# Attention from the fifth tile on: high and low halves of a head in one product, quadrants added at eviction

## The chip, the cores and the metric

The kernel runs on one core of one Trainium2 chip. The metric is the device time of one execution in microseconds. A core has a matrix engine (TensorE, in the rows PE, with PEld for its weight loads), a vector engine (VectorE, DVE), a scalar engine (ScalarE, ACT), GpSimd (POOL) and a sync engine that issues transfers (SyncE, SP). They run their own instruction streams and wait for one another through semaphores. Matrix products land in PSUM, which has eight banks of 2 KB per partition.

## What is computed

Three layers over 2304 tokens (4 sequences of 576) with 512 channels. The inputs of the dense layer come in 64-bit words. Cut to what matters here:

```python
scores = (q @ k.T) / 8            # 8 heads of 64 channels, causal window of 128 tokens
scores = where(mask, scores + bias, -1e9)
attn = exp(scores - scores.max(-1))
attn = attn / (attn.sum(-1) + 1e-9)
x = heads_to_channels(attn @ v)   # 2304 x 512
r = maximum(x @ w_in, 0)          # dense layer, 2048 hidden columns
x = (s * r * r + b) @ w_out
# then 8 experts of 1024 columns, the best two of each token, weighted and summed
```

The change concerns `attn @ v`.

## The kernel before

Attention works in 18 tiles of 128 tokens. A tile has four units, one for each pair of heads. A unit's tokens look at their own block of 128 keys and, if the sequence has one, the block ahead of it, so that most units have two key blocks and the first of a sequence has one (`blocks`). For each unit `qk` computes scores and probabilities, `ptr` transposes the probabilities into the PSUM tile `tp` and copies them to SBUF, and `av` multiplies them by V. `evac` copies the product, which has channels on the partitions, into `xh` and `xl`, from which the dense layer reads.

Operands that need precision are kept as a high part `h` and a low part `l` in a reduced 32-bit type, and a product is made of three: high by high, high by low, low by high. From tile 4 on (`FX`) attention does so for V: `split_v` makes the high part of V on ScalarE (L309) and the low part on GpSimd, into blocks `vb`; `ptr` makes the high probabilities `pth` on ScalarE (L366) and the low ones `ptl` on VectorE (L368). In `av` the stationary operand is a pair of heads, 128 channels of V, and the moving operand is the 256 probabilities of both heads of one block. Half of the result is of no use: the channels of head 0 under the probabilities of head 1 and the reverse.

```python
mm += [(so, h, th)] if ti < FX else [(so, h, th), (so, h, tl), (so, l, th)]
```

So one unit takes six matmuls of 128x256 (L382), three where it has one block. One PSUM bank `av` holds two units; there is one such bank. After the second unit `evac` takes the two useful quadrants: two copies on ScalarE (L391, 64x256) give `xh`, and two subtractions on VectorE (`low`, L118) give `xl`.

The dense layer works in nine chunks of 256 tokens, each in pairs of 256 hidden columns: `l1` (L457) reads `xh` and `xl` and makes `hp`, VectorE and ScalarE turn it into `gh` and `gl` (L465, L469), `l2` (L500) sums into the PSUM tiles `o`. Attention is woven between these matmuls. `marks` sets the pace: tiles 0 and 1 stand ahead of the first chunk, tiles 2 and 3 ahead of the second, and each chunk that follows must find its two tiles done. The first two chunks run in halves, and tiles 4 and 5 have four pairs of hidden columns to run in; later ones have a whole chunk. Two names of the router also stand in the orders below: `lp` (L532, gate) and `r_u`, `r_e` (its softmax).

Instructions are written in this program order. A scheduler in the framework sorts them for each engine when the program is built, by priority, estimated durations and free buffers; on the chip each engine runs its row in that order. The buffers that matter: PSUM has one bank for `tp`, one for `av`, two for scores `sp`, two for `hp`, two for `o`. In SBUF `pth` has one buffer, `ptl` two, which the weight conversion's `z` (L125) shares, `vb` has four, and the pool `u2k` has two for `g` of the dense layer and, in the first chunk, for the residual tiles `x` (L510) and `xt`.

The conversion of the dense layer's weights from 64-bit words (`conv1` to `conv3`, tiles `w`, `z`, `wih`, `wil`, `woh`, `wol`) runs on ScalarE and VectorE in the first 138 us.

## Time and profile before

| what | us |
|---|---|
| median of three runs | 1101.35 |
| lowest and highest | 1100.8, 1103.46 |
| the profiled execution | 1102.03 |
| its span (first to last instruction) | 1100.3 |
| TensorE busy in the span | 1063.5 |
| VectorE busy | 587.6 |
| ScalarE busy | 538.0 |
| GpSimd busy | 283.7 |

The profile is of one execution. Its time is 1.7 us more than its span. Busy time is the sum of instructions in work; TensorE's matmuls overlap, so what a matmul takes from the span is the distance from its start to the next start, not its length in the row. A line such as L382 is that of the kernel above.

### The profile page before, as it was taken

What the parts mean: (1) busy time and instruction counts of PE and PEld (TensorE: products, weight loads), DVE (VectorE), ACT (ScalarE), POOL (GpSimd) and SP (SyncE); (2) the same over time, 40 slices, a digit from 0 to 9 for tenths busy, and PEclk for the clock granted to TensorE, in tenths of its full rate; (3) what the DMA queues carried; (4) which work ended last, traced back from release to release, by engine and by line L of the source; (5) the groups of instructions that cost most, each with busy time, mean ns of one, the idle gap of its engine ahead of it and who ended that gap; (6) DMA issues with size and microseconds to landing.
All of it is one profiled execution on the core that took longest, in us unless ns stands there. A gap on an engine that the chain in (4) does not pass through costs nothing. (4 is left out here: it accounts for less than half of the span.)

```text
span 1100.3 us, 16721 instructions
## 1 busy us (share of the span) xinstructions
PE 1063.5 (97%) x6219; PEld 914.9 (83%) x6219; DVE 587.6 (53%) x1531; ACT 538.0 (49%) x1080; POOL 283.7 (26%) x265
## 2 busy tenths in 40 slices
PE   6899989999999999999999899999999999999997
PEld 3678878998999999999998787878888888887875
DVE  5999968767566676757455345242241421515140
ACT  4897667566566666555452145252342422424241
POOL 2000225324214242323001523323213032140223
PEclk9999999999999999999999999999999999999999
DMA  8965421011001111010233436455344343444212
GB/s 236 276 186 177 142 88 55 30 30 54 25 29 30 49 31 49 21 49 2 90 122 96 87 92 183 113 139 110 86 126 84 115 113 70 127 93 136 48 14 38
DMA packets 53779, 100.16 MB, mean 91 GB/s; under 512 B 12340, under 2 KB 23736, under 8 KB 53688
## 3 DMA queue, kind: packets, MB, share of 16 engines
q1 hardware_dynamic: 41784, 76.87, 22.8%
q0 software_dynamic: 11904, 22.08, 10.8%
q8 instruction: 57, 0.93, 0.4%
q14 instruction: 34, 0.28, 0.1%
HBM read 78.28 MB, written 23.78 MB: 93 GB/s over the span
## 5 line engine op out<-in xcount | busy, mean ns | idle before, releaser
L457 PE MATMUL hp<-xh,wih 128*128 128x256 f32 x576 | 168.0, 292 | 0.7 <-ACT wih L139 0.7
L457 PE MATMUL hp<-xl,wih 128*128 128x256 f32 x576 | 164.4, 285 | 0.4 <-DVE xl L118 0.4
L457 PE MATMUL hp<-xh,wil 128*128 128x256 f32 x576 | 164.2, 285 | 0.4 <-DVE wil L118 0.4
L785 PE MATMUL ys<-woh,wih 128*128 128x512 f32 x512 | 160.1, 393 | 0.2 <-ACT wih L732 0.2
L717 POOL DMA_INDIRECT xg<-x2d,ix x48 | 47.7, 993 | 316.8 <-PE xp L57 277.5
L804 ACT ACTIVATE yo<-ys,ls 128x512 f32<-128x512 f32 x46 | 31.2, 689 | 178.2 <-issue 147.2
L500 PE MATMUL o<-woh,gh 128*128 128x512 f32 x288 | 116.6, 406 | 0.0
L500 PE MATMUL o<-woh,gl 128*128 128x512 f32 x288 | 113.7, 395 | 0.2 <-DVE gl L469 0.2
L457 PEld LDWEIGHTS hp<-xh,wih 128*128 128x128 f32 x576 | 110.2, 191 | 3.8 <-ACT wih L139 1.1
L457 PEld LDWEIGHTS hp<-xl,wih 128*128 128x128 f32 x576 | 110.4, 192 | 3.2 <-DVE xl L118 1.9
L500 PE MATMUL o<-wol,gh 128*128 128x512 f32 x288 | 112.8, 392 | 0.0
L457 PEld LDWEIGHTS hp<-xh,wil 128*128 128x128 f32 x576 | 110.4, 192 | 1.0 <-DVE wil L118 0.6
L785 PEld LDWEIGHTS ys<-woh,wih 128*128 128x128 f32 x512 | 95.1, 188 | 19.2 <-ACT wih L732 0.5
L740 PE MATMUL hp<-xh,wih 128*128 128x512 f32 (+1 forms) x288 | 107.9, 375 | 3.2 <-DVE wil L733 1.3
L740 PE MATMUL hp<-xl,wih 128*128 128x512 f32 (+1 forms) x288 | 107.5, 373 | 2.1 <-PEq L766 0.9
L740 PE MATMUL hp<-xh,wil 128*128 128x512 f32 (+1 forms) x288 | 106.7, 370 | 1.2 <-PEq L766 0.6
L785 PE MATMUL ys<-woh,wil 128*128 128x512 f32 x256 | 100.0, 391 | 0.1
L805 POOL DMA_INDIRECT out_dram<-yo,ix x48 | 79.9, 1665 | 67.5 <-ACT yo L804 53.7
L118 POOL TENSOR_TENSOR ql<-rows,qd 64x256 fp32r<-64x256 f32 x52 | 39.5, 760 | 199.8 <-PE sp L325 138.9
L732 ACT ACTIVATE wih<-hp 128x512 fp32r<-128x512 f32 x64 | 37.9, 593 | 104.4 <-PE hp L740 104.2
L337 ACT ACTIVATE pr<-pr,st 128x256 f32<-128x256 f32 (+1 forms) x144 | 70.3, 489 | 29.6 <-DVE st L335 27.5
L733 DVE SCALAR_TENSOR_TENSOR wil<-hp,wih 128x512 fp32r<-128x512 f32 x64 | 44.1, 689 | 74.1 <-ACT wih L732 74.0
(181 smaller groups left out, 2269.6 us busy)
## 6 DMA issues: line engine op xcount, KB each, us to landing
raw<-in_moe_w_dram SPq DMA_DIRECT2D x64, 512.0 KB, 4.1
w<-in_moe_w_in_dram SPq DMA_DIRECT2D x16, 512.0 KB, 4.5
w<-in_moe_w_out_dram SPq DMA_DIRECT2D x16, 512.0 KB, 4.3
x2d<-x SPq DMA_DIRECT2D x22, 256.0 KB, 2.0
rows<-in_q_dram SPq DMA_DIRECT2D x18, 256.0 KB, 2.7
out_dram<-zero SPq DMA_DIRECT2D x18, 256.0 KB, 4.6
rows<-in_k_dram SPq DMA_DIRECT2D x16, 256.0 KB, 2.6
rows<-in_v_dram SPq DMA_DIRECT2D x14, 256.0 KB, 2.6
```

The costliest lines, as they stand in the source:

```text
L118: eng.tensor_tensor(out=dl, in0=x, in1=dh.bitcast(F32), op=OP.subtract)
L337: x_ = nc.scalar.activation(t[:, c], t[:, c], AF.Exp, bias=st[:, 0, e:e + 1], scale=-1.0, accum_out=st[:, 1, e:e + 1])
L457: nc.tensor.matmul(h[:, fi, :], a[:, kk, fs], bb[:, kk, cs], start=m == 0, stop=m == 3 * KD - 1)
L500: nc.tensor.matmul(o, a[:, ts], bb[:, f, :], start=i == i0 and m == 0, stop=i == i1 and m == 5)
L717: nc.gpsimd.indirect_dma_start(out=x, out_offset=None, in_=x2d, in_offset=bass.IndirectOffsetOnAxis(ap=LS[e, j][1], axis=0))
L732: nc.scalar.activation(dh, p, AF.Relu)
L733: nc.vector.scalar_tensor_tensor(out=dl, in0=p, scalar=0.0, in1=dh.bitcast(F32), op0=OP.max, op1=OP.subtract)
L740: nc.tensor.matmul(o, a[:, kk, fs], xt(z, c0, c1)[:, kk, :], start=m == 0, stop=m == 3 * KD - 1)
L785: nc.tensor.matmul(o, ht(z, j * 128, j * 128 + 128)[:, f // 2, f % 2], b[:, f, :], start=m == 0, stop=m == 3 * KF - 1)
L804: nc.scalar.activation(yo, y, AF.Copy, scale=wt)
L805: st = nc.gpsimd.indirect_dma_start(out=out, out_offset=bass.IndirectOffsetOnAxis(ap=ix, axis=0), in_=yo, in_offset=None, bounds_check=NT ...
```

## The change

From tile 4 on the operands are laid out by head. A block `vb` holds for each head its 64 high and 64 low columns next to one another, and a block `ptz` holds for each head the 128 high and 128 low probabilities next to one another. One matmul of a head and a key block then has 128 stationary columns (high and low V) and 256 moving ones (high and low probabilities). Its result has four quadrants: high by high, high by low, low by high, and low by low. A unit has two heads, so it takes four such matmuls with two blocks and two with one. It fills a PSUM bank by itself.

The eviction adds the quadrants. ScalarE copies two of them (L401, L402) into a scratch tile `ev`, VectorE adds high by high to the first (L403), then adds the sums into the first columns of the same PSUM bank, one head to each half of the partitions (L405, two instructions), ScalarE copies the result to `xh` (L406), and VectorE makes `xl` (L118). This runs for each unit. Low by low is among the quadrants that are added; before it was left out.

`ev` comes out of the pool `u2k`. `ptz`, the early tiles' `pth` and the conversion's `z` share three buffers. V's blocks are two of 4 KB in place of four of 2 KB, and the early tiles load their V in pairs into one such block.

```diff
-        z = x["z"] = ap.tile([128, 512], F32, name="z", tag="ptl", bufs=2).rearrange("p (k c) -> p k c", k=lo.shape[1])
+        z = x["z"] = ap.tile([128, 512], F32, name="z", tag="pz", bufs=3).rearrange("p (k c) -> p k c", k=lo.shape[1])
...
-            t = vblock(F32).rearrange("p (h d) -> p h d", d=D)
+            if ti % 2 == 0:
+                V["raw"] = vblock(F32).rearrange("p h z d -> p (h z d)").rearrange("p (a h d) -> p a h d", a=2, d=D)
+            t = V["raw"][:, ti % 2]
...
-        return ap.tile([128, DM], dt, name="vb", tag="vb", bufs=4)
+        return ap.tile([128, H, 2, D], dt, name="vb", tag="vb", bufs=2)
 
     def halve_v(ti, r):
-        V[ti] = (vblock(F32R), vblock(F32R))
-        nc.scalar.activation(V[ti][0], r, AF.Copy)
-        low(nc.gpsimd, V[ti][1], r, V[ti][0])
+        V[ti] = vblock(F32R)
+        nc.scalar.activation(V[ti][:, :, 0, :], r, AF.Copy)
+        low(nc.gpsimd, V[ti][:, :, 1, :], r, V[ti][:, :, 0, :])
...
-        th = ap.tile([128, 2, 2, 128], F32 if ti < FX else F32R, name="pth", tag="pth")
-        tl = ap.tile([128, 2, 2, 128], F32R, name="ptl", tag="ptl", bufs=2) if ti >= FX else None
         pt = P.pop(u)
         bl = blocks(ti)
         for so in bl:
             for e in range(2):
                 turn(tp[:, so, e, :], pt[e][:, so * 128:so * 128 + 128])
-        s = slice(0, 2) if len(bl) == 2 else slice(bl[0], bl[0] + 1)
-        nc.scalar.activation(th[:, s], tp[:, s], AF.Copy)
-        if tl is not None:
-            nc.vector.tensor_tensor(out=tl[:, s], in0=tp[:, s], in1=th[:, s].bitcast(F32), op=OP.subtract)
-        PT[u] = (th, tl)
+        if ti < FX:
+            th = ap.tile([128, 2, 2, 128], F32, name="pth", tag="pz", bufs=3)
+            s = slice(0, 2) if len(bl) == 2 else slice(bl[0], bl[0] + 1)
+            nc.scalar.activation(th[:, s], tp[:, s], AF.Copy)
+            PT[u] = th
+            return
+        PT[u] = {}
+        for so in bl:
+            x = PT[u][so] = ap.tile([128, 2, 2, 128], F32R, name="ptz", tag="pz", bufs=3)
+            nc.scalar.activation(x[:, :, 0], tp[:, so], AF.Copy)
+            nc.vector.tensor_tensor(out=x[:, :, 1], in0=tp[:, so], in1=x[:, :, 0].bitcast(F32), op=OP.subtract)
...
     def av(u):
         ti, p = divmod(u, NP)
-        th, tl = PT.pop(u)
-        if p % 2 == 0:
-            AV[ti, p // 2] = pp.tile([128, 2, 2, 128], F32, name="av", tag="av")
-        o = AV[ti, p // 2]
-        mm = []
-        for so in blocks(ti):
-            h, l = V[ti if so == tiles[ti].so else ti - 1]
-            mm += [(so, h, th)] if ti < FX else [(so, h, th), (so, h, tl), (so, l, th)]
-        for i, (so, a, bb) in enumerate(mm):
-            nc.tensor.matmul(o[:, p % 2], a[:, p * 128:(p + 1) * 128], bb[:, so], start=i == 0,
-                             stop=i == len(mm) - 1)
+        t = PT.pop(u)
+        if ti >= FX or p % 2 == 0:
+            AV[ti, p if ti >= FX else p // 2] = pp.tile([128, 2, 2, 128], F32, name="av", tag="av")
+        o = AV[ti, p if ti >= FX else p // 2]
+        bl = blocks(ti)
+        vs = [V[ti if so == tiles[ti].so else ti - 1] for so in bl]
+        n = len(bl) - 1
+        if ti < FX:
+            for i, so in enumerate(bl):
+                nc.tensor.matmul(o[:, p % 2], vs[i].rearrange("p h d -> p (h d)")[:, p * 128:(p + 1) * 128], t[:, so],
+                                 start=i == 0, stop=i == n)
+            return
+        for e in range(2):
+            for i, so in enumerate(bl):
+                nc.tensor.matmul(o[:, e], vs[i][:, 2 * p + e], t[so][:, e], start=i == 0, stop=i == n)
 
     def evac(ti, ph):
         o = AV.pop((ti, ph))
+        d = (ti * 128 + CH) % RING
+        if ti >= FX:
+            ev = u2k("ev").rearrange("p (z e q) -> p z e q", z=2, e=2)[0:64]
+            nc.scalar.activation(ev[:, 0], o[0:64, :, 1, :], AF.Copy)
+            nc.scalar.activation(ev[:, 1], o[64:128, :, 0, :], AF.Copy)
+            nc.vector.tensor_tensor(out=ev[:, 0], in0=o[0:64, :, 0, :], in1=ev[:, 0], op=OP.add)
+            for e in range(2):
+                nc.vector.tensor_tensor(out=o[64 * e:64 * e + 64, 0, 0, :], in0=ev[:, 0, e], in1=ev[:, 1, e], op=OP.add)
+            nc.scalar.activation(xh[:, ph, d:d + 128], o[:, 0, 0, :], AF.Copy)
+            low(nc.vector, xl[:, ph, d:d + 128], o[:, 0, 0, :], xh[:, ph, d:d + 128])
+            return
         ps = slice(2 * ph, 2 * ph + 2)
...
-            if p2 % 2:
-                add(lambda t2=t2, ph=p2 // 2: evac(t2, ph), need=(t2 * 128) // CH - 2,
+            if p2 % 2 or t2 >= FX:
+                add(lambda t2=t2, ph=p2 if t2 >= FX else p2 // 2: evac(t2, ph), need=(t2 * 128) // CH - 2,
```

On TensorE, where tile 4 ends and tile 5 begins (`o` is the dense layer's sum, `hp` its hidden values and `gh`, `gl` the same later, `sp` scores, `tp` transposes, `lp` the gate), before:

```order
L57 MATMUL tp<-ident,pr 128x128 x4
L457 MATMUL hp<-xh,wil 128x256
L457 MATMUL hp<-xh,wih 128x256
L457 MATMUL hp<-xl,wih 128x256
L457 MATMUL hp<-xh,wil 128x256
L500 MATMUL o<-woh,gh 128x512
L500 MATMUL o<-wol,gh 128x512
L500 MATMUL o<-woh,gl 128x512
L500 MATMUL o<-woh,gh 128x512
L500 MATMUL o<-wol,gh 128x512
L500 MATMUL o<-woh,gl 128x512
L382 MATMUL av<-pth,vb 128x256
```

and after:

```order
L394 MATMUL av<-ptz,vb 128x256 x4
L553 MATMUL lp<-wg,xt 128x16 x4
L57 MATMUL tp<-ident,pr 128x128 x4
L394 MATMUL av<-ptz,vb 128x256 x4
L325 MATMUL sp_119<-k_1518,qd 128x256
L327 MATMUL sp_119<-k_1518,ql 128x256
L521 MATMUL o<-woh,gh 128x512
```

Before, these rows stand between the last matmul of tile 4's last product and the first one of tile 5's first, which is the last row here: four transposes, four first-layer and six second-layer matmuls. After, the first row is tile 4's last product and the fourth tile 5's first: four gate matmuls and four transposes part them.

On VectorE, the second unit of tile 10 in the steady stretch (`xl` is the low part for the dense layer, `g` and `gl` are its hidden values), before:

```order
L469 SCALAR_TENSOR_TENSOR gl<-g,sb_c,gh 128x512
L535 COPY lg<-lp 128x16
L118 TENSOR_TENSOR xl<-av,xh 64x2x128 x2
L535 COPY lg<-lp 128x16
L465 SCALAR_TENSOR_TENSOR g<-hp,g 128x512
L547 TENSOR_SCALAR r_u<-r_e 128x16
L549 SCALAR_TENSOR_TENSOR r_e<-r_u,r_e 128x16
L368 TENSOR_TENSOR ptl<-tp,pth 128x512
```

and after:

```order
L556 COPY lg<-lp 128x16
L403 TENSOR_TENSOR ev<-av,ev 64x256
L405 TENSOR_TENSOR av<-ev 64x128 x2
L118 TENSOR_TENSOR xl<-av,xh 128x128
L556 COPY lg<-lp 128x16
L486 SCALAR_TENSOR_TENSOR g<-hp,g 128x512
L568 TENSOR_SCALAR r_u<-r_e 128x16
L570 SCALAR_TENSOR_TENSOR r_e<-r_u,r_e 128x16
L375 TENSOR_TENSOR ptz<-tp,ptz 128x2x128
```

Two subtractions have become three additions and one subtraction in a row of the engine, and the low probabilities `ptl` of both blocks have become two instructions `ptz`.

## Rows read from the trace of the kernel before

**Rows 1.** The page's busy times: busy us (share) x instructions of each engine
```profile
PE 1063.5 (97%) x6219; PEld 914.9 (83%) x6219; DVE 587.6 (53%) x1531; ACT 538.0 (49%) x1080; POOL 283.7 (26%) x265
```

**Rows 2.** Stretches: length, busy us (count) per engine PE PEld DVE ACT POOL, clock, DMA, GB/s
```profile
0.00:140.00 140.00, 124.55 (x651) 96.41 (x652) 121.73 (x315) 103.42 (x234) 19.91 (x32) 0.98 0.68 201
140.00:196.00 56.00, 52.10 (x359) 46.09 (x360) 41.46 (x143) 37.82 (x89) 22.20 (x22) 1.00 0.23 73
196.00:504.00 308.00, 306.58 (x2148) 283.04 (x2147) 203.90 (x667) 184.76 (x417) 99.14 (x100) 1.00 0.12 34
```

**Rows 3.** Timeline, TensorE: start, length us, engine, line, operation, tiles, elements
```profile
264.02 0.39 PE L500 MATMUL o<-woh,gl 128*128 128x512 f32 x1
264.25 0.28 PE L382 MATMUL av<-pth,vb 128*128 128x256 f32 x1
...
264.85 0.28 PE L382 MATMUL av<-pth,vb 128*128 128x256 f32 x1
264.97 0.28 PE L457 MATMUL hp<-xh,wih 128*128 128x256 f32 x1
```

**Rows 4.** Groups by line and shape: xcount | busy us, mean ns | idle before, releaser
```profile
L368 DVE TENSOR_TENSOR ptl<-tp,pth 128x512 fp32r<-128x512 f32 x52 | 35.8, 689 | 32.3 <-ACT pth L366 31.4
L366 ACT ACTIVATE pth<-tp 128x512 fp32r<-128x512 f32 x52 | 31.0, 596 | 53.0 <-PE tp L57 52.9
L118 DVE TENSOR_TENSOR xl<-av,xh 64x256 fp32r<-64x256 f32 x72 | 30.2, 420 | 13.0 <-ACT xh L391 12.2
L391 ACT ACTIVATE xh<-av 64x256 fp32r<-64x256 f32 x72 | 26.9, 374 | 5.0 <-PE av L382 4.1
L125 ACT ACTIVATE z<-w 128x512 f32<-128x512 f32 x32 | 21.5, 671 | 10.0 <-DMA w<-in_moe_w_in_dram 5.3 <-DVE w L133 3.6 <-DMA w<-in_moe_w_out_dram 1.1
L368 DVE TENSOR_TENSOR ptl<-tp,pth 128x256 fp32r<-128x256 f32 x4 | 1.7, 420 | 1.3 <-ACT pth L366 1.3
L366 ACT ACTIVATE pth<-tp 128x256 fp32r<-128x256 f32 x4 | 1.5, 382 | 4.8 <-PE tp L57 4.8
```

**Rows 5.** Timeline, evacuations of the steady stretch; [idle before <-releaser] in us
```profile
256.69 0.28 PE L382 MATMUL av<-pth,vb 128*128 128x256 f32 x1
...
258.62 0.77 ACT L391 ACTIVATE xh<-av 64x256 fp32r<-64x256 f32 x2
...
259.41 0.86 DVE L118 TENSOR_TENSOR xl<-av,xh 64x256 fp32r<-64x256 f32 x2 [2.18 <-ACT xh L391]
...
378.41 0.28 PE L382 MATMUL av<-pth,vb 128*128 128x256 f32 x1
...
439.64 0.28 PE L382 MATMUL av<-pth,vb 128*128 128x256 f32 x1
...
439.96 0.77 ACT L391 ACTIVATE xh<-av 64x256 fp32r<-64x256 f32 x2
...
440.76 0.86 DVE L118 TENSOR_TENSOR xl<-av,xh 64x256 fp32r<-64x256 f32 x2 [0.57 <-ACT xh L391]
```

**Rows 6.** Stretches in the place where tiles 4 and 5 run
```profile
148.00:160.00 12.00, 11.81 (x87) 10.75 (x85) 8.32 (x21) 5.35 (x14) 2.51 (x3) 1.00 0.14 45
160.00:172.00 12.00, 12.00 (x88) 10.97 (x89) 8.56 (x33) 10.20 (x25) 5.67 (x5) 1.00 0.13 45
172.00:184.00 12.00, 11.60 (x82) 10.03 (x82) 11.67 (x57) 7.53 (x21) 4.55 (x5) 1.00 0.09 24
```

**Rows 7.** Timeline, TensorE: a group of gate matmuls and the matmul that follows it
```profile
159.71 0.96 PE L532 MATMUL lp<-wg,xt 128*128 128x16 f32 x8
160.52 0.36 PE L382 MATMUL av<-ptl,vb 128*128 128x256 f32 x1
```

**Rows 8.** Timeline, VectorE and ScalarE: a residual addition, a copy of tile 4
```profile
145.40 0.69 DVE L510 TENSOR_TENSOR x<-o,x 128x512 f32<-128x512 f32 x1 [2.15 <-DMA x<-x2d]
...
147.86 0.36 ACT L391 ACTIVATE xh<-av 64x256 fp32r<-64x256 f32 x1
```

**Rows 9.** DMA issues: tiles, queue, operation xcount, KB each, us from issue to landing
```profile
x2d<-x SPq DMA_DIRECT2D x22, 256.0 KB, 2.0
```

More of the change, by code (lines that the diff above doesn't have):

```diff
@@ L294, in split_v @@
     def split_v(ti):
-        r = rows.pop(("v", ti)).rearrange("p h d -> p (h d)")
+        r = rows.pop(("v", ti))
         if ti < FX:
-            V[ti] = (r, r)
+            V[ti] = r
         else:
             if ti == FX and tiles[ti].prev:
-                halve_v(ti - 1, V[ti - 1][0])
+                halve_v(ti - 1, V[ti - 1])
             halve_v(ti, r)
@@ L387, in evac @@
         ps = slice(2 * ph, 2 * ph + 2)
-        d = (ti * 128 + CH) % RING
         for e in range(2):
```

## The prediction

> **What bounds the kernel now.** I read the busy table first: TensorE (PE) works 1063.5 us of a span of 1100.3 us, with VectorE (DVE) at 53% and ScalarE (ACT) at 49% [rows 1]. That is an average over stages with different limits (the expert stage, the latter half, has no attention), so the second view is the table by stretches [rows 2]. From 196 to 504 us, where attention is woven into the dense layer, PE works 306.58 of 308 us, DVE 203.90 (66%) and ACT 184.76 (60%), at a granted clock of 1.00: nothing but the number of matmuls sets the time there. From 0 to 140 us DVE is the full engine (121.73 of 140); it converts weights, and PE has 15 us of gaps. From 140 to 196 us PE has 3.9 us of gaps.
>
> The third view is the timeline of one attention product [rows 3]. Six matmuls start between 264.25 and 264.85, the next one at 264.97: (264.97 − 264.25)/6 = 0.12 us for one 128x256 matmul. The 0.28 us in the row is its latency; the starts are what counts on a full engine. The 128x512 matmul ahead stands 0.23 us.
>
> The fourth is the evacuation of a finished pair of units [rows 5]: the last product starts at 439.64 and ends at 439.92, ACT takes 439.96 to 440.73, DVE 440.76 to 441.62. The chain is 1.70 us, with 0.04 us or so at each change of engine. The same product one chunk earlier starts at 378.41: a chunk is 61.2 us. The longest such chain of the steady stretch starts at 256.69, where ACT comes 1.65 us late: 256.97 to 260.27, 3.30 us.
>
> The fifth is the dense place [rows 6]. Tiles 4 and 5 must be through before the third chunk of the dense layer starts, at about 181 us. From 172 to 184 us DVE works 11.67 of 12 us and PE 11.60, from 160 to 172 ACT 10.20 and PE 12.00: three engines are nearly full together, nowhere else after 140 us.
>
> **The change part by part.**
>
> Matmuls removed. The low-probability product ran 108 times: twice for each of 52 two-block units, once for each of four single-block ones (x52 and x4 of line L368 [rows 4]). A two-block unit goes from 6 matmuls to 4, a single-block one from 3 to 2: 2 × 52 + 4 = 108 fewer, of the same 128x256 shape, each with its weight load. At 0.12 us: 108 × 0.12 = 13.0 us. Sixteen of them belong to tiles 4 and 5, the other 92 to later tiles, nearly all after 184 us where PE is full, so they count whole.
>
> The Trainium skill, page "TensorE: Matmul & The Clock Gate", section "Back-to-back issue gap", has about 81 ns for a matmul of 128 columns and 131 ns for one of 512 in a sustained stream of weight loads and matmuls. A straight line between them gives an estimate of 98 ns at 256 columns and a gain of 108 × 0.098 = 10.5 us, so a time 2.5 us longer than mine. The rows contradict it at both sizes (0.12 at 256, 0.23 at 512 [rows 3]), so the measurement decides.
>
> Vector work added, per two-block unit [rows 4]. Transposed probabilities: DVE two 128x256 for one 128x512, 2 × 0.420 − 0.689 = +0.151 us; ACT 2 × 0.382 − 0.596 = +0.168. Evacuation: the 128x128 form is not in the trace, so I take it from the slope of 128x512 to 128x256: ACT 0.382 − (0.596 − 0.382)/2 = 0.275, DVE 0.420 − (0.689 − 0.420)/2 = 0.286, both estimates. The 64x256 copy is 0.374 on ACT, 0.420 on DVE, and before there is one of each per unit. After: ACT 2 × 0.374 + 0.275 − 0.374 = +0.649, DVE 0.420 + 2 × 0.286 + 0.286 − 0.420 = +0.858. Together DVE +1.01 us and ACT +0.82 us per unit. With 8 units in a chunk of 61 us, DVE goes from 66% to 79% and ACT from 60% to some 71%. In the steady stretch PE's full row covers that.
>
> The longer chain. After a unit's product stand 0.75 (two ACT copies) + 0.42 + 3 × 0.286 (DVE) + 0.275 (ACT) = 2.30 us of work in series plus hand-offs, some 2.4 us against 1.70, and it is now due for each unit, not each second one: there is one product bank, and the next unit's product waits for its release. Queued behind a waiting DVE addition stand the router's copy and the squares of the dense layer (order of VectorE above); TensorE's dense matmuls wait for the latter.
>
> Place by place. In the steady stretch the changed order puts 4.9 to 9 us of PE work between one product and the next (the matmuls between them, counted by shape, at 0.12 and 0.23 us), against 2.4: free. At a chunk's end the dense layer needs the last evacuation some 2.7 us after the product (before 2.1 us against 1.7), and the second-layer matmuls of the third chunk's first pair follow 2.3 us behind their first layer, where 6.5 us stood before. I put 2.5 us on all of these; bounds 0 (all cover holds) and 6 (0.5 us at each of 12 tiles).
>
> At the dense place the cover is gone. Between the last product of tile 4 and the first of tile 5 the changed order has four gate matmuls and four transposes, where transposes and ten dense matmuls stood (order of TensorE above). The gate takes 160.52 − 159.71 = 0.81 us [rows 7], the transposes less than 4 × 0.12: some 1.2 us, against a chain of 2.4. DVE is full there [rows 6], so four units of tile 5 bring 4 × 1.0 = 4.0 us that find no room, and the last evacuation ends 0.7 later: 4.7. Sixteen matmuls, 1.9 us, are not gained since PE is not last there; six second-layer matmuls, which stood behind tile 6's first product, are filler that can be drawn forward, 6 × 0.23 = 1.4 us. 4.7 + 1.9 − 1.4 = +5.2 us. Bounds: 0 when DVE's other work shifts behind 184 us; 10.3 when each of tile 5's four units stands for a loaded chain, 3.3 − 1.2 = 2.1 us, and nothing is gained: 8.4 + 1.9.
>
> Shared buffers. The new scratch shares its two buffers with the residual tiles: the addition at 145.40 [rows 8] ends at 146.09, its store lands 2.0 us later [rows 9], about 148.1, where the copy for tile 4's second unit stood at 147.86: 0.3 us, inside the 5.2. The early weight conversion shares three buffers with the probabilities, where it had two: it had waited 3.6 us for DVE [rows 4]. I take −1 us, near the nearer end since DVE stays the full engine; bounds −3.6 and +2 (a conversion step put behind probabilities).
>
> V's split writes the same bytes by the same two instructions into one block per tile, four blocks of 2 KB became two of 4 KB: nothing, hidden by the rows loaded a tile ahead.
>
> Sum: −13.0 + 5.2 + 2.5 − 1.0 = −6.3 us. The profiled execution took 1102.0 us, span 1100.3; that gives 1095.7. The median of the runs, 1101.35, lies 0.7 lower, hence 1095.0.
>
> **The rivals.**
>
> Full gain. The dense place costs nothing: 1101.35 − 13.0 = 1088.3. For it: DVE has 3.4 us of room from 160 to 172 and 3.7 from 148 to 160 [rows 6], and a scheduler may have used it. Against: ACT is full where DVE is not, and the two alternate in the chain.
>
> The gain eaten at the dense place. With the upper bound there: −13.0 + 10.3 + 2.5 − 1.0 = −1.2, so 1100.1, within 0.3%. For it: the product order with 1.2 us of cover. That the change would not do what it says belongs here too; the order, with 108 matmuls fewer, leaves it hardly a chance.
>
> Slower: the loaded chain. The evacuation changes engine between ACT and DVE three times and each change stands behind what its queue holds. ACT and DVE rows of 0.6 to 0.7 us are common [rows 4]; with one of them ahead of each of the five steps the chain is 2.4 + 5 × 0.7 = 5.9 us. In a steady tile two of the distances between products are only 5.1 to 5.5 us: a chain of 6 costs 1.6 us a tile, over 12 tiles 19 us: −6.3 + 19 = +13, some 1114. It is slower by 0.3% from a chain of about 5.6 us on (9.6 us over 12 tiles, 0.8 us a tile). For it: DVE at 79% also stands still while it waits for ACT in its row. Against: of the chains before, the worst loaded one is 3.30 us against 1.70 [rows 5]; the same factor makes 4.7 out of 2.4, still short of 5.1.
>
> **How the numbers follow.** A measurement of this kernel tells 0.3%, 3.3 us, from no change: faster is below 1098.0, slower above 1104.7. The forecast case (1092 to 1098) has 0.44, the full gain 0.17, the eaten gain 0.26 (1098 to 1104), the loaded chain 0.13. Predicted is the likeliest, 1095.0. The range runs from 1088.0, the full gain, to 1104.5, the eaten gain with its bounds; about 0.18 stays outside. Faster 0.44 + 0.17 = 0.61, same 0.26, slower 0.13.
>
> **What would show it.** After: 108 fewer attention matmuls, their starts still 0.12 us apart, and a full PE between 200 and 500 us; a chunk of the dense layer some 1.9 us shorter (16 matmuls) — right for the first step. PE idle of 4 to 7 us more between 150 and 190 us, released by ACT or DVE of the evacuation — right for the second. DVE at 79% in the steady stretch, the 128x128 forms near 0.28 us. Wrong if PE shows more than 0.5 us idle per tile in front of the attention products after 200 us (the loaded chain), if the additions that write to PSUM take far longer than 0.29 us, or if the stretch up to 140 us moved by more than 3 us.

## The result, and the profile after

| | before | after |
|---|---|---|
| median, us | 1101.5 | 1112.4 |
| lowest to highest | 1100.8 to 1103.5 | 1112.0 to 1118.4 |
| profiled execution | 1102.0 | 1118.4 |
| its span | 1100.3 | 1116.5 |

The changed kernel is slower: ratio 1.0108, 95% interval 1.0077 to 1.0139. That lies above the range given. The profiled execution is the slowest of those after, 6 us over the median; it serves for where the time goes, and the medians for how much. Where those 6 us lie in it, no run shows, so a delay read from this trace can be too long by up to 6 us.

One sentence of the change's description has to be put right: low by low is computed but not added. ScalarE copies high by low and low by high, VectorE adds these to high by high, and the fourth quadrant stays where it is.

The page's busy times after, as [rows 1]:

```profile
PE 1069.7 (96%) x6111; PEld 911.4 (82%) x6111; DVE 642.8 (58%) x1751; ACT 573.3 (51%) x1244; POOL 281.3 (25%) x265
```

TensorE has 108 matmuls fewer (6219 to 6111), VectorE 220 instructions more and 55 us more work, ScalarE 164 and 35 us. By stretches, as [rows 2] (length, then busy us and count of PE, PEld, DVE, ACT, POOL, then clock, DMA share, GB/s):

```profile
0.00:140.00 140.00, 124.07 (x608) 94.14 (x609) 118.85 (x307) 101.32 (x226) 19.54 (x32) 0.96 0.68 200
140.00:196.00 56.00, 50.35 (x308) 43.57 (x306) 41.63 (x156) 37.44 (x102) 11.91 (x13) 0.91 0.19 60
196.00:504.00 308.00, 298.91 (x2029) 270.64 (x2030) 244.65 (x826) 206.57 (x530) 103.23 (x105) 0.99 0.11 35
```

PE was full from 196 to 504 us (306.58 of 308); now it has 9 us of gaps there. From 140 to 196 us it passes 308 matmuls where it passed 359, at a granted clock of 0.91.

To see where the kernel falls behind, take one instruction that both programs have in the same place: ScalarE's first copy of `hp`, one for each pair of hidden columns. Timeline of ScalarE, before, for the eleventh and nineteenth pair:

```profile
127.28 0.67 ACT L464 ACTIVATE g<-hp,sb_c 128x512 f32<-128x512 f32 x1
...
198.65 0.69 ACT L464 ACTIVATE g<-hp,sb_c 128x512 f32<-128x512 f32 x1 [2.11 <-PE hp L457]
```

and after, the same two, and the 41st and 49th, one chunk apart:

```profile
128.89 0.69 ACT L485 ACTIVATE g<-hp,sb_c 128x512 f32<-128x512 f32 x1
...
213.72 0.69 ACT L485 ACTIVATE g<-hp,sb_c 128x512 f32<-128x512 f32 x1 [0.74 <-PE hp L478]
...
383.44 0.69 ACT L485 ACTIVATE g<-hp,sb_c 128x512 f32<-128x512 f32 x1 [1.22 <-PE hp L478]
...
444.41 0.69 ACT L485 ACTIVATE g<-hp,sb_c 128x512 f32<-128x512 f32 x1 [1.20 <-PE hp L478]
```

At the eleventh pair the changed kernel is 1.6 us behind, at the nineteenth 15.1: 13.5 us are lost between the two, around the dense place. A steady chunk takes 444.41 − 383.44 = 61.0 us, as long as the 61.2 us before, though it has 16 matmuls fewer. So there are two losses: one around the dense place, and a gain of about 10 us that never came in the steady stretch. These marks are used below: **early** is the delay at the eleventh pair, **dense** that at the nineteenth, **late** that at the 69th (573.3 us before), and the **chunk** is the mean of four from the 25th to the 57th pair (60.95 us before, 61.56 after). All are starts of that same row in each kernel's trace, against the kernel before. Each trace is of one execution, which lies within 3.5 us of its kernel's median but for three: 6.0 us over it in the changed kernel, 7.0 in ptr_ord, 4.5 in from9.

**The dense place.** The second unit of tile 4 on the timeline, its last products and the first copy of its eviction:

```profile
149.37 0.62 PE L394 MATMUL av<-ptz,vb 128*128 128x256 f32 x3
...
157.05 0.63 PE L57 MATMUL tp<-ident,x 128*128 128x128 f32 x4 [0.30 <-DVE ptz L375]
...
157.71 0.38 ACT L401 ACTIVATE ev<-av 64x256 f32<-64x256 f32 x1 [1.74 <-PE tp L57]
```

The copy starts 7.7 us after the products end at 149.99. ScalarE has other work put ahead of it, and for the last 1.74 us stands idle. What it waits for then is no product but a transpose, L57: the residual tile `x` that holds the scratch buffer is still to be turned for the gate. The third unit's copy starts 6.7 us after its product, released by the gate's matmuls (L553), which read the turned tile. TensorE's longest waits from 140 to 205 us are not those of a product for its bank (0.3 us in all), but two of the first-layer matmuls for the eviction's `xh` (3.5 us in all). The granted clock falls after PE's gaps. Stretches of 5 us, and then the timeline of TensorE in them:

```profile
170.00:175.00 5.00, 2.81 (x15) 2.30 (x14) 4.03 (x13) 3.93 (x10) 3.26 (x3) 0.81 0.01 2
175.00:180.00 5.00, 4.72 (x16) 3.88 (x17) 4.07 (x14) 4.75 (x13) 1.27 (x1) 0.51 0.37 105
```

```profile
177.82 0.63 PE L521 MATMUL o<-woh,gh 128*128 128x512 f32 x1
178.24 0.63 PE L521 MATMUL o<-wol,gh 128*128 128x512 f32 x1
...
180.16 0.39 PE L521 MATMUL o<-wol,gh 128*128 128x512 f32 x1
180.39 0.39 PE L521 MATMUL o<-woh,gl 128*128 128x512 f32 x1
```

PE is idle for 2.2 of 5 us, and in the next stretch the granted clock is 0.51, the level of 1.2 GHz: a 128x512 matmul takes 0.42 us from start to start at 177.82, and 0.23 again at 180.16. In that one stretch (1 − 0.51) × 5 = 2.4 us of full clock are missing.

**The steady stretch.** One unit of tile 12, all engines, from its transposes to its products:

```profile
405.01 0.60 PE L57 MATMUL tp<-ident,pr 128*128 128x128 f32 x4
...
405.97 0.38 ACT L374 ACTIVATE ptz<-tp 128x256 fp32r<-128x256 f32 x1
...
407.15 0.41 DVE L375 TENSOR_TENSOR ptz<-tp,ptz 128x256 fp32r<-128x256 f32 x1
...
407.19 0.28 ACT L406 ACTIVATE xh<-av 128x128 fp32r<-128x128 f32 x1 [0.83 <-DVE av L405]
...
407.93 0.39 ACT L374 ACTIVATE ptz<-tp 128x256 fp32r<-128x256 f32 x1
...
408.72 0.28 PE L394 MATMUL av<-ptz,vb 128*128 128x256 f32 x1
...
409.15 0.41 DVE L375 TENSOR_TENSOR ptz<-tp,ptz 128x256 fp32r<-128x256 f32 x1
...
409.62 0.63 PE L394 MATMUL av<-ptz,vb 128*128 128x256 f32 x3 [0.39 <-DVE ptz L375]
```

and one before, the same way:

```profile
388.14 0.60 PE L57 MATMUL tp<-ident,pr 128*128 128x128 f32 x4
...
388.84 0.60 ACT L366 ACTIVATE pth<-tp 128x512 fp32r<-128x512 f32 x1 [0.31 <-PE tp L57]
...
389.47 0.69 DVE L368 TENSOR_TENSOR ptl<-tp,pth 128x512 fp32r<-128x512 f32 x1
...
391.86 0.28 PE L382 MATMUL av<-pth,vb 128*128 128x256 f32 x1
```

Before, the probabilities are ready 1.42 us after the transposes (388.74 to 390.16), and the order of PE leaves 3.12 us until the product. After, the first block's are ready after 1.95 us (405.61 to 407.56) and the second block's after 3.95 (to 409.56). The order leaves 3.1 us to the unit's first matmul (408.72) and some 3.5 to the second, which reads the second block: that one waits. In a chunk before, this path took 1.36 to 2.37 us in all units; after, 1.75 to 3.96, and two units of eight come late, by 0.4 to 0.6 us each. Both vector engines are late in the unit shown: ScalarE makes the second copy at 407.93, behind an `xh` for which it had stood idle 0.83 us, waiting for VectorE's addition. How full VectorE is there is seen in slices of the chunk, after and then before:

```profile
403.80:408.90 5.10, 5.10 (x40) 4.84 (x38) 4.95 (x31) 3.09 (x10) 1.29 (x2) 1.00 0.00 0
408.90:414.00 5.10, 4.71 (x36) 3.93 (x36) 4.96 (x17) 2.80 (x8) 2.45 (x3) 1.00 0.16 53
```

```profile
386.10:391.20 5.10, 5.10 (x43) 4.98 (x42) 4.38 (x29) 2.43 (x8) 0.53 (x1) 1.00 0.02 5
```

VectorE is at 4.95 of 5.1 us there, 31 instructions in one slice: the router's small steps stand in the same row with the additions and the `ptz`. Before, the fullest slice of a chunk had 4.44.

The prices of the new instructions, by line and shape (count, busy us, mean ns, idle before):

```profile
L375 DVE TENSOR_TENSOR ptz<-tp,ptz 128x256 fp32r<-128x256 f32 x108 | 45.1, 417 | 13.9 <-ACT ptz L374 12.9
L374 ACT ACTIVATE ptz<-tp 128x256 fp32r<-128x256 f32 x108 | 41.1, 381 | 32.0 <-PE tp L57 15.8 <-DVE ptz L375 15.4
L405 DVE TENSOR_TENSOR av<-ev 64x128 f32<-64x128 f32 x112 | 36.9, 330 | 3.6
L403 DVE TENSOR_TENSOR ev<-av,ev 64x256 f32<-64x256 f32 x56 | 23.0, 411 | 13.1 <-ACT ev L402 12.8
L402 ACT ACTIVATE ev<-av 64x256 f32<-64x256 f32 x56 | 21.3, 381 | 0.7
L401 ACT ACTIVATE ev<-av 64x256 f32<-64x256 f32 x56 | 20.4, 365 | 9.0 <-PE av L394 5.5 <-PE tp L57 1.7 <-PE lp L553 1.6
L118 DVE TENSOR_TENSOR xl<-av,xh 128x128 fp32r<-128x128 f32 x56 | 16.0, 286 | 8.6 <-ACT xh L406 8.3
L406 ACT ACTIVATE xh<-av 128x128 fp32r<-128x128 f32 x56 | 15.5, 276 | 50.6 <-DVE av L405 50.4
```

### The profile page after: what moved, and what is told of

Same layout as the page of the kernel before. It is cut to its first block, busy times and chain, and to the rows that moved or that the text cites. A ratio compares the mean times of both kernels' runs of the same rounds, so it can differ in the third digit from the quotient of the medians.

```text
span 1116.5 us, 16939 instructions
## 1 busy us (share of the span) xinstructions
PE 1069.7 (96%) x6111; PEld 911.4 (82%) x6111; DVE 642.8 (58%) x1751; ACT 573.3 (51%) x1244; POOL 281.3 (25%) x265
## 3 DMA queue, kind: packets, MB, share of 16 engines
q0 software_dynamic: 11904, 22.08, 10.6%
## 5 line engine op out<-in xcount | busy, mean ns | idle before, releaser
L118 POOL TENSOR_TENSOR ql<-rows,qd 64x256 fp32r<-64x256 f32 x52 | 38.9, 748 | 136.2 <-PE sp L327 117.6
```

The costliest lines, as they stand in the source:

```text
L118: eng.tensor_tensor(out=dl, in0=x, in1=dh.bitcast(F32), op=OP.subtract)
```

## The experiments

Each was timed beside the kernel before. The marks are delays against the kernel before, in us.

| kernel | median | ratio, 95% interval | early | dense | late | chunk |
|---|---|---|---|---|---|---|
| before | 1101.5 | | 0 | 0 | 0 | 60.95 |
| changed | 1112.4 | 1.0077 to 1.0139 | +1.6 | +15.1 | +16.6 | 61.56 |
| ev_pz | 1109.0 | 1.0050 to 1.0084 | −1.6 | +7.6 | +7.4 | 61.22 |
| ptr_ord | 1123.3 | 1.0168 to 1.0212 | +2.2 | +17.5 | +26.4 | 62.66 |
| from9 | 1106.6 | 1.0027 to 1.0060 | +2.2 | +8.2 | +7.9 | 61.15 |
| upto8 | 1119.6 | 1.0154 to 1.0188 | +0.9 | +13.2 | +11.9 | 60.72 |
| ctl_old | 1107.7 | 1.0043 to 1.0077 | −0.2 | +4.9 | +5.3 | 61.01 |
| no_hl | 1094.3 | 0.9924 to 0.9969 | −2.6 | +2.5 | −7.9 | 59.36 |
| one_copy | 1123.1 | 1.0179 to 1.0216 | −0.6 | +10.9 | +22.1 | 63.13 |
| one_copy_x | 1115.7 | 1.0107 to 1.0146 | +0.4 | +9.0 | +17.9 | 63.09 |
| no_add | 1091.0 | 0.9895 to 0.9928 | +0.4 | +0.8 | −9.0 | 59.38 |
| old_split | 1106.8 | 1.0033 to 1.0067 | +2.1 | +4.8 | +5.7 | 61.04 |
| old_pz | 1103.0 | 1.0014 to 1.0036 | −0.1 | +0.9 | +1.3 | 61.00 |
| tags_ev | 1110.4 | 1.0068 to 1.0105 | −2.8 | +9.2 | +10.3 | 61.51 |
| nopp | 1136.7 | 1.0278 to 1.0345 | −0.3 | +16.8 | +35.4 | 64.27 |
| nopp_pz | 1128.2 | 1.0204 to 1.0262 | +1.7 | +11.2 | +30.5 | 64.55 |
| pool_pz | 1133.9 | 1.0256 to 1.0316 | +1.0 | +12.5 | +36.9 | 65.72 |
| dummy | 1119.9 | 1.0135 to 1.0189 | −0.9 | +6.0 | +17.3 | 63.16 |
| tiny | 1118.7 | 1.0129 to 1.0179 | +1.8 | +11.0 | +18.0 | 62.34 |
| dummy_act | 1103.3 | 1.0011 to 1.0034 | +0.9 | +3.1 | +1.0 | 60.77 |

**The scratch buffer (ev_pz).**

```diff
-            ev = u2k("ev")...
+            ev = ap.tile([128, 512], F32, name="ev", tag="pz", bufs=3)...
```

> The changed kernel with one edit: the scratch tile of the eviction comes from the three buffers of the probabilities, no longer from the two that it shared with the residual tiles of the first chunk. Theory A (shared scratch): in the changed kernel the first eviction copy of tile 4's second and third unit began 7.7 and 6.7 us after the product because the scratch buffer was still held by a residual tile; without that the dense place loses some 10 us less, so 1100 to 1104 us, and these two copies begin within 1.5 us of the product. Theory B (full vector engine): DVE has no room at the dense place whatever the buffer, so 1110 to 1114 us.

1109.0: neither. The two copies now follow the product within 1 us (153.76 after 153.50 for the third unit). That is worth 3.4 us of the median, and the delay at the nineteenth pair halves in the traces. But 9 of the 13.5 us between the first two marks stay, and the chunk gains nothing.

**Which tiles (from9, upto8).** The old three products for tiles 4 to 8, and for 9 to 17.

```diff
+    NEW = range(9, 18)      # or range(4, 9)
+        if ti not in NEW: th, tl = ... both from tag "pz"; three products
```

> The change from tile 9 on alone; tiles 4 to 8 make three products with the high and low parts as before (all out of the same three shared buffers). 68 matmuls fewer, worth 68 x 0.12 = 8.2 us where TensorE is full. If the loss sits at the dense place of tiles 4 and 5 (A, B), nothing is lost here. If the steady stretch gives the gain whole: 1093.5 us. If it gives it back in small waits, as the equal chunk periods of the two profiles (61.2 and 61.3 us) say: 1100 to 1102 us.

> The change for tiles 4 to 8 alone; tiles 9 to 17 make three products as before. If the loss sits at the dense place and the steady stretch gains nothing: as the changed kernel, 1111 to 1114 us. If the steady stretch gains and its later tiles are left out: 8 us more, about 1120. If the loss is spread over all tiles (the loaded chain): about 1106 us.

From tile 9 on, the change neither gains nor loses: the delay is +8.2 when it begins, +7.9 at the end. That the gain is given back is right, but the kernel carries 8 us from the stretch ahead, where it makes the old products. With the change up to tile 8, the delay is 13.2 at the nineteenth pair and then falls by 1.5 as far as the new tiles go; after that it does not move. So the case of the expectation that meets its median, 1119.6, is not the one that its trace shows: the marks follow the first case, and another 4 us are lost behind the 69th pair, in the expert stage (span 1116.4, 16.1 over before). Why there, I can't say.

**The storage alone (ctl_old, old_pz).** All products old.

```diff
+    NEW = range(0, 0)       # ctl_old: V's blocks and the three shared buffers as in the change
-    th = ap.tile(..., tag="pth"); tl = ap.tile(..., tag="ptl", bufs=2)
+    th, tl: tag="pz", bufs=3   # old_pz: this on the kernel before, and nothing else
```

> The old three products for all tiles, with the storage of the change alone: V's parts in one block per tile, the early tiles' V in pairs, the probabilities' high and low parts and the conversion's scratch out of three shared buffers. Theory D (the new storage by itself re-deals the early stage and costs there, as the run with the change from tile 9 on was 8 us behind before it came to tile 9): 1106 to 1110 us. Rival (storage costs nothing, the loss there was the change's): 1100 to 1102.5 us.

> The kernel before with one edit: high and low probabilities and the conversion's scratch share three buffers, where the high ones had one and the low ones shared two with the scratch. V's blocks are as before. Theory D1 (the shared buffers make the 7 us that the storage alone cost): 1106 to 1109 us. Rival D2 (V's blocks in pairs make it): 1100 to 1102.5 us.

The new storage by itself costs the old products 7 us (theory D), 2.4 of them by the shared buffers; the rest I put down to V's blocks, which I had priced at nothing, but no run has V's blocks alone. In the trace 4.9 us of it arise ahead of the nineteenth pair; the delay then stays constant to 0.4 us as far as the 69th, and the rest comes in the expert stage, which no edit touches. Going back to the old buffers on the changed kernel did not give it back:

> The changed kernel with the buffers of the kernel before for scratch and probabilities: the early high probabilities and each unit's first block out of one buffer, the conversion's scratch, each unit's second block and the eviction's scratch out of two. It goes with the run that took the eviction's scratch out of the residual tiles' pool (1109.0). If the three shared buffers make the early loss (D1): 4 to 7 us less, 1102 to 1105 us. If not: 1107 to 1111 us.

1110.4, not better than 1109.0. Early it is 2.8 us ahead, and it loses 12 at the dense place. The parts don't add up, as each edit lets the scheduler place the first 200 us anew: no_hl, next, loses 5 us between the first two marks though it only leaves out matmuls. So a difference of a few us in the early or dense mark is no price of the edited part.

**The price of a matmul (no_hl).** The kernel before without high V by low probabilities.

```diff
-            mm += ... else [(so, h, th), (so, h, tl), (so, l, th)]
+            mm += ... else [(so, h, th), (so, l, th)]
```

> The kernel before without the product of the high V and the low probabilities: 108 matmuls fewer, everything else of the vector engines as before. What is left out is that product alone. Theory: TensorE's issue is the bound and each matmul is worth 0.12 us, 13.0 us in all: 1088 to 1090 us. Rival (other engines hold the pace of a chunk at 61 us, which would explain that the changed kernel's chunk is as long with 16 matmuls fewer): 1097 us or more.

From the nineteenth to the 69th pair it gains 2.5 + 7.9 = 10.4 us, and the chunk is 59.36, 1.6 us shorter: the price of 0.12 us holds where nothing is put in its place. It loses 5 us ahead of that, so that 1094.3 meets neither theory's figure. It is not true that other engines hold the chunk at 61 us.

**The copies of the probabilities (ptr_ord, one_copy, one_copy_x, old_split).** Two copies, then two subtractions; one copy and one subtraction for both blocks, for which residual tiles of later chunks move to the three shared buffers; the same with those of the first chunk moved too; and the split copies in the run with the old products.

```diff
-        for so in bl: copy(so); subtract(so)
+        for so in bl: copy(so)          # ptr_ord
+        for so in bl: subtract(so)
+        copy(all); subtract(all)        # one_copy, tile "ptz" of 4 KB from tag "rb"
```

> The changed kernel with the two ScalarE copies of the transposed probabilities written one behind the other, and the two VectorE subtractions after them, so that ScalarE no longer waits for VectorE between its copies. Theory C (the split transposed copy makes the stalls of the steady stretch, 0.4 to 1 us a chunk in front of the products): 2 to 5 us less than the changed kernel, 1107 to 1110 us. Theories A and B: no matter, 1111 to 1114 us.

> The changed kernel with the transposed probabilities of both blocks copied by one ScalarE instruction and made low by one VectorE instruction, into one tile of 4 KB (two buffers, which the residual tiles of later chunks gave up; these use the three 2 KB buffers). Theory C (two alternating pairs of instructions make the probabilities late for the product, 0.5 to 0.8 us at one or two units a chunk): the waits of the products go, the chunk falls from 61.3 to about 60 us, 6 to 8 us in all: 1104 to 1107 us. Rival E (the longer eviction keeps VectorE behind, whatever the copies do): 1110 to 1114 us.

> As the run with one copy, and the residual tiles of the first chunk out of the 2 KB buffers too, so that the eviction's scratch shares its two buffers with the dense layer's squares alone. Theories A and C together: some 3 us below the run with one copy, 1100 to 1104 us. If only A matters: 1108 to 1110 us. If neither: 1110 to 1114 us.

> The run with the old products and the new storage, with the high and the low probabilities made block by block (two ScalarE and two VectorE instructions in turn, as in the change). Nothing else is added. Theory C: products wait some 0.5 us at two units of a chunk, which adds 5 to 8 us to 1107.7: 1112 to 1116 us. Theory E: the split alone costs nothing as long as VectorE has room, 1107 to 1109 us.

Theory C falls. Splitting the copies costs nothing with the old products in the new storage (1106.8 against 1107.7), ptr_ord is 11 us slower than the changed kernel where C had it faster, and joining the copies makes the steady stretch worse (chunks of 63.1 us; the moved residual tiles are in that too). There the waits of the products shrink little (3.4 to 2.4 us between 210 and 560 us), and transposes wait for VectorE's last router step on their PSUM bank, 8.9 us in one_copy, where it was 2.6 in the changed kernel.

**The sum left out (no_add).** The two copies to the scratch and the three additions are gone; the four products stay.

```diff
-            nc.scalar.activation(ev[:, 0], ...); nc.scalar.activation(ev[:, 1], ...)
-            nc.vector.tensor_tensor(out=ev[:, 0], ...)
-            for e in range(2): nc.vector.tensor_tensor(out=o[64 * e:...], ...)
```

> The changed kernel without the sum of the quadrants: the two ScalarE copies to the scratch tile and the three VectorE additions are left out, xh and xl are made from the first quadrant's columns of the bank as they stand. Per unit 0.75 us of ScalarE and 1.0 us of VectorE less; the four products and the split copies of the probabilities stay. Theory E (the eviction's work delays VectorE's queue, and so the probabilities and the transposes): the waits of the steady stretch go, and the chunk falls to about 59.4 us, 10 us in all, and more at the dense place: 1095 to 1101 us. Theory C (the split copies of the probabilities alone make the products wait): the chunk stays near 61 us, 1106 to 1110 us.

1091.0, lower than either theory. Its stretch from 205 to 500 us, and that of the changed kernel under it:

```profile
205.00:500.00 295.00, 293.09 (x2037) 268.90 (x2036) 207.89 (x693) 178.46 (x446) 97.50 (x100) 1.00 0.12 36
```

```profile
205.00:500.00 295.00, 288.20 (x1965) 260.87 (x1964) 236.00 (x799) 197.02 (x508) 94.37 (x97) 0.99 0.11 33
```

PE is full again, the chunk is 59.38, and the dense place costs 0.3 us, with the same split copies, the same four products and the same storage. TensorE's products wait 0.2 us for their probabilities between 210 and 560 us, where they waited 3.4. So the sum of the quadrants costs 1112.4 − 1091.0 = 21.4 us, the scheduler's new order for the early stage included, and without it the kernel gains 9.5 of the 13.0 us. The storage's 7 us are therefore no fixed price either: this kernel has the same storage and falls only 3.5 us short.

**Chain or amount (nopp, nopp_pz, pool_pz, dummy, tiny, dummy_act).** First, the hand-offs cut from three to one: ScalarE makes both copies and `xh`, then VectorE adds and subtracts in SBUF. Then the same with other buffers, and with one addition on GpSimd.

```diff
+            for e in range(2): nc.scalar.activation(xh[64 * e:...], o[0:64, e, 0, :], AF.Copy)
-                out=o[64 * e:64 * e + 64, 0, 0, :]
+                out=full[64 * e:64 * e + 64, 0:128]
-            nc.scalar.activation(xh[...], o[:, 0, 0, :], AF.Copy)
```

> The changed kernel with the eviction in another order of hand-offs and nearly the same work: ScalarE makes the two copies to the scratch tile and both heads' xh (from the high by high quadrant) one behind the other, then VectorE makes its three additions and the subtraction one behind the other, in SBUF; the corrections go into xl alone. VectorE's four instructions stay, ScalarE has two 64x128 copies in place of one 128x128 (0.27 us more a unit). One change of engine in place of three, and nothing is written back to the product's bank. Theory F (the hand-offs cost: each engine stands in its row while it waits for the other): most of the 21 us that the sum costs come back, 1095 to 1101 us. Theory G (the amount of work on VectorE, 80% busy, costs): 1108 to 1114 us.

> As the run with one hand-off, and the scratch tile out of the three buffers of the probabilities, not out of the residual tiles' pool. With the shared scratch's part (3.4 us between the changed kernel and its run with the other buffers): under theory F 1092 to 1099 us, under theory G 1105 to 1110 us.

> As the run before this, with the addition of the two small quadrants on GpSimd (64x256, in SBUF), so that VectorE has two additions of 64x128 and one subtraction: 0.4 us a unit less on VectorE, one more change of engine. Theory G: 3 to 6 us below the run with one hand-off and the same buffers. Theory F: no gain, or up to 3 us more for the further hand-off.

All three are far slower, and both theories miss. In nopp, VectorE's first addition now waits for all of ScalarE's four copies on that bank (24.8 us in all, by line):

```profile
L406 DVE TENSOR_TENSOR ev<-av,ev 64x256 f32<-64x256 f32 x56 | 23.2, 414 | 25.8 <-ACT xh L405 24.8 <-PE hp L480 0.4
```

and at the chunk's end the dense layer waits for `xl`, since the additions of two SBUF operands are held up (last section); VectorE's and TensorE's timeline:

```profile
383.14 2.33 DVE L408 TENSOR_TENSOR ev<-ev 64x128 f32<-64x128 f32 x2
...
385.85 0.39 PE L480 MATMUL hp<-xl,wih 128*128 128x256 f32 x1 [2.29 <-DVE xl L118]
```

So they measure another eviction with waits of its own, not the number of hand-offs. Then the two put apart: no_add with the same work on constants that nobody waits for; the whole chain on 8 of 128 columns; and of the unconnected work ScalarE's two copies alone.

```diff
+            nc.scalar.activation(ev[0:64, 0], cw[0:64, 0], AF.Copy)      # dummy, dummy_act; cw: weights
+            nc.scalar.activation(ev[0:64, 1], cw[64:128, 0], AF.Copy)
+            nc.vector.tensor_tensor(out=ev[64:128, ...], in0=cw[...], in1=cw[...], op=OP.add)  # dummy, three
-            nc.scalar.activation(ev[:, 0], o[0:64, :, 1, :], AF.Copy)
+            nc.scalar.activation(ev[:, 0, :, 0:8], o[0:64, :, 1, 0:8], AF.Copy)                # tiny, all five
```

> The run without the sum of the quadrants, with the same vector work put back, unconnected: per unit two ScalarE copies of 64x256 and three VectorE additions (64x256 and two of 64x128), on constant data, into the scratch tile, that nobody waits for and that wait for no product. xh and xl are made from the first quadrant's columns as they stand. Theory G (the amount of vector work costs): near the changed kernel, 1107 to 1114 us. Theory F (the sum costs because it stands in a chain between the product and the next buffers, whatever its amount): near the run without it, 1091 to 1098 us.

> The changed kernel with the sum of the quadrants on 8 of 128 columns of each head alone: all seven instructions of the eviction, their waits and their three changes of engine stay, the five of the sum are short. The other columns keep the first quadrant. Theory F (the hand-offs cost): 1105 to 1112 us. Theory G (the amount of work costs): 1091 to 1099 us.

> As the run with unconnected work, without its three VectorE additions: the two ScalarE copies of constant data into the scratch tile stay, and the tile's share of the residual tiles' pool with them. If it is VectorE's work that costs (1.07 us a unit, on an engine that is full around the router's steps): near the run without the sum, 1091 to 1097 us. If ScalarE's work or the shared pool does it: 1105 us or more.

Unconnected work is enough to lose the gain: 1119.9, more than with the sum itself. But it is not lost by the same waits. Between 210 and 560 us TensorE's products wait 3.1 us for their probabilities, as in the changed kernel, but its transposes 10.6 us for the router's last step, where it was 2.6 there. Nor is the work quite the same: all of its additions have two SBUF operands, and 17 of 168 were held up, 11.5 us in all, against 7 of 112 and 3.8 us (last section). The stretches of dummy_act and dummy:

```profile
205.00:500.00 295.00, 289.14 (x1986) 262.08 (x1985) 203.39 (x690) 199.20 (x515) 94.52 (x97) 1.00 0.12 36
```

```profile
205.00:500.00 295.00, 280.93 (x1896) 255.20 (x1896) 233.27 (x774) 192.81 (x493) 94.54 (x93) 0.98 0.11 32
```

With ScalarE's copies alone (ACT 178 to 199 us, VectorE as without) the chunk goes from 59.38 to 60.77: most of the steady gain is lost already, 12.3 us of the median: ScalarE makes the high probabilities and is in the same path, and the products' waits for these grow from 0.2 to 3.7 us. VectorE's part adds 16.6. So the expectation that it would be VectorE alone was wrong, though the scratch buffer in the copies' price was not parted from ScalarE's time. The run on 8 columns, 1118.7, decides less than it was meant to: its short instructions still hold 61% of VectorE's time (0.164 + 2 × 0.246 us in place of 0.411 + 2 × 0.330), it has held-up additions at the chunk's end, and its transposes wait 7.2 us for the router's last step.

What stays open is how the 21.4 us of the real sum divide between its amount and its chain, and why V's blocks moved the early stage.

## Why the prediction was wrong

- **108 matmuls at 0.12 us, 13.0 us: right.** No_hl and no_add, each with those matmuls gone and little or nothing put in, gain 1.6 us a chunk. Between the nineteenth and the 69th pair 88 of the matmuls are gone, 10.6 us at that price, and the two gain 10.4 and 9.8 there.
- **The vector work: right.** VectorE +1.01 us a unit was forecast; by the rows 0.411 + 2 × 0.330 + 0.286 + 2 × 0.417 less the 1.109 of before is +1.08. ScalarE +0.82 was forecast, and the rows make it +0.81. VectorE's share of the steady stretch is 80% (79 forecast).
- **The steady stretch, 2.5 us, bounds 0 to 6: this is the first step that failed.** It took some 11 to 12 us: the 88 matmuls were worth 9.8 to 10.6 there, and the changed kernel lost 1.5 more. The step compared the eviction's chain with the distance to the next product. That comparison holds for most units. In one unit a chunk the loaded chain rose to 5.1 to 5.3 us, over the 4.7 that the prediction allowed, and took all of the distance, as here:

```profile
485.98 0.64 PE L394 MATMUL av<-ptz,vb 128*128 128x256 f32 x4
...
491.61 0.27 DVE L118 TENSOR_TENSOR xl<-av,xh 128x128 fp32r<-128x128 f32 x1
...
492.26 0.39 PE L394 MATMUL av<-ptz,vb 128*128 128x256 f32 x1 [0.48 <-DVE ptz L375]
```

  The chain ends at 491.88, when TensorE has been idle for 0.1 us, and the product waits until 492.26, for its probabilities. The path that mattered was the one into the product, transposes to copies to subtractions, with 3.1 us of order and 1.4 used before. It was priced as work on an engine (+0.15, +0.17 us), not as a path behind queues that had become longer. "PE's full row covers that" was said of a mean share of 79%; the slices of 5 us, in which VectorE had 4.4 of 5.1 already, were not read. How the loss divides between the amount of the added work and the waits inside its chain stays open.
- **The dense place, 5.2 us, bounds 0 to 10.3: mis-sized, and its wait was another.** Between the marks 13.5 us were lost although 20 of the matmuls were gone there, so that the term measures 15.9 us in this trace. Some of that is the new storage, with which the old products lost 5 us between the same marks. The prediction had tile 5's products wait for their bank; what waited longest was the dense layer for `xh`. The shared scratch was looked at and priced at 0.3 us, by the store's landing; the residual tile is held beyond that, until the gate's transposes, and the copies came 7.7 and 6.7 us after their products; without that the median is 3.4 us lower. The rest of this term stays open. The halved clock that follows PE's gaps was not in the sum.
- **Shared buffers −1 us, V's blocks nothing: wrong.** The storage alone cost 7.0 us with the old products.
- **The loaded chain as a rival, 1114: right in sign, and near in size by luck, for its mechanism is not what was seen.** In the steady stretch no product's wait ended with the release of its bank. Its remark that VectorE stands still in its row while it waits was nearer to the cause than its price. The sign that was set for it, over 0.5 us lost per tile ahead of the products, came about (some 1.1 us by their starts in a chunk of two tiles), with another wait.

By the Trainium skill, page "TensorE: Matmul & The Clock Gate", section "Back-to-back issue gap", the prediction estimated a gain of 10.5 us, not 13.0, from a line between the page's two figures. No_add's 9.5 us of median doesn't tell the two apart, since part of it is lost early. But the starts in the rows stay 0.12 and 0.23 us apart at full clock, and the 10.4 and 9.8 us of no_hl and no_add lie nearer to 88 × 0.12 = 10.6 than to the estimate's 88 × 0.098 = 8.6.

## What to carry to other kernels

A full engine with a fixed order has slack only where the order left some: before adding work to a half-idle engine, follow every path through it that ends at the full engine, with the distance in the order against the path's length under load, in slices as short as the path, not the mean share. Work that nobody waits for can cost as much as work in the path, as it stands in a queue ahead of work that is waited for. A scratch tile from a shared pool is held for as long as the other tenants' last reader takes, and that reader is to be looked up.

## What the runs showed of the hardware

An addition on VectorE with both operands in SBUF was held up when it began while a two-operand instruction of GpSimd (TENSOR_TENSOR) was running. VectorE and then GpSimd in the changed kernel:

```profile
173.56 1.32 DVE L405 TENSOR_TENSOR av<-ev 64x128 f32<-64x128 f32 x1
```

```profile
173.47 1.26 POOL L118 TENSOR_TENSOR vb<-rows,vb 128x512 fp32r<-128x512 f32 x1 [0.73 <-POOL ql L118]
```

The addition takes 1.32 us where its median is 0.30, and ends 0.15 us after GpSimd's. The same holds for an addition of 8 columns, median 0.17 us, in the run on 8 columns:

```profile
375.88 1.15 DVE L405 TENSOR_TENSOR av<-ev 64x8 f32<-64x8 f32 x1
```

```profile
375.48 1.52 POOL L118 TENSOR_TENSOR vb<-rows,vb 128x512 fp32r<-128x512 f32 x1 [1.69 <-ACT vb L311]
```

In the changed kernel eight of the 112 additions L405 began so, and seven of them took 0.53 to 1.32 us, 3.8 us more in all; five that began beside a GpSimd DMA kept their 0.30 us. In nopp 12 of 112 were held up, for up to 1.83 us. VectorE instructions with one operand in PSUM were not: of L403, `xl` and `ptz` together 31 began beside such a GpSimd instruction, and none took over 0.43 us. The Trainium skill, page "GPSIMD Engine Reference", section "1. Specifications", names two SBUF inputs of a VectorE instruction as a case of contention with GpSimd; these rows agree, and give its price here, up to 1.0 us in the changed kernel.
